# One of four tiles of exponentials folded on GpSimd before VectorE adds it

## The chip, the cores and the metric

The kernel runs on one core of one Trainium2 chip. A core has a matrix engine (TensorE, PE in the profile), and VectorE (DVE), ScalarE (ACT) and GpSimd (POOL), each with an instruction queue of its own that it works off in order; a further queue (SP) only issues transfers (DMA). The metric is the device time of one execution in microseconds. "The profile" is a recording of one execution with the start and the duration of every instruction.

## The reference

An input `x` of 2048 tokens by 512 is normalised. From it come an attention over cached keys and values (32 heads of 128, 2048 queries, 2048 keys) and a small network that makes a gate; the output is `x + attention * silu(network)`.

```python
def _A_ref(x, k_cache, v_cache, wq, wo):
    q = (x @ wq).reshape(B, Sq, H, Dh).transpose(0, 2, 1, 3)
    scores = jnp.einsum("bhqd,bhkd->bhqk", q, k_cache) * (Dh ** -0.5)
    p = _softmax(scores, axis=-1)
    o = jnp.einsum("bhqk,bhkd->bhqd", p, v_cache)
    return o.transpose(0, 2, 1, 3).reshape(B, Sq, H * Dh) @ wo

xn = _layernorm(x, axis=-1)
s = _A_ref(xn, A_k_cache, A_v_cache, A_wq, A_wo)
g = _silu(_B_ref(xn, B_w1, B_w2, B_w3, B_w4))
return x + s * g
```

What matters here is the denominator of the softmax: for every query the sum of the exponentials over all 2048 keys.

## The kernel before

The network runs first, in about the first 155 us. The rest is the attention, cut into 128 *units*: one head by one block of 512 queries (8 groups of 4 heads, 4 blocks of queries per group, the heads of a group next to each other). A unit has 8 *slots*, `n = 8 * u + p` with `p` the slot in unit `u`. A slot multiplies two blocks of 128 keys with the queries (`s_slot`, L425; out comes a 128x1024 block of scores, keys in the partitions), and ScalarE writes their exponentials (L436) into half of a tile `pT` of 128 x 4 x 512. So a unit has four such tiles, the second full after slot 3, the third after slot 5, the fourth after slot 7. There are six buffers for them. Ten slots behind, `pv_slot` multiplies the tiles with the values.

**The sums.** VectorE adds the four tiles into one accumulator `acc` of the same shape: tiles 0 and 1 in slot 4 (`add_first`, L442), tile 2 in slot 6 (`add_next`, L447), tile 3 in slot 0 of the next unit (L447 as well). The accumulator is then halved twice (`fold`, L451, to 1024 columns; `fold_last`, L455, to 512), turned by a transposing DMA (`turn`, L480), summed along the columns (`turned_sums`, L485), inverted (L491), and sent through DRAM to all partitions (`dr`, then `rb`). In slot 7 of the second unit after it, `norm` (L509) multiplies the attention's output in PSUM with it.

**The queries.** From unit 16 on the queries of two heads (a *pair*: an even and an odd unit) are made with seven smaller products in place of eight (`product`, L367), whose results VectorE combines in four steps, `q_part` 0 to 3 (L413, L416, L418, L421). They share one PSUM tile per pair, `ps_q`: after `q_part` 1 and 2, in slots 0 to 1 of the odd unit, the next two products (slots 4 and 5) write into the same tile, and `q_part` 3 in slot 6 reads it.

**The output product.** `wo_slot` multiplies finished heads with `wo` into a PSUM bank `ps_wo`, which `wo_post` (L571, or L564 and others for the last groups) adds to a running result on VectorE; the bank is then free for the next one. In the last groups VectorE also scales and adds up results (L537, L542, L567, L580, L582).

**What sets the order.** Every instruction is pinned in the order of the program's text, so that each engine's queue is fixed by the loop over `n` (L932 to L1002). In slot 0 of a unit VectorE's queue holds: `turned_sums`, the reciprocal, `add_next(u - 1, 3)`. Then, in slot 0 or 1: `q_part(1)`, `fold`, `q_part(2)`, `fold_last` in odd units; `fold`, `q_part(0)`, `fold_last` spread over slots 0 to 2 in even ones. GpSimd's queue holds only work of the first 155 us, among it the `rs` powers (L194). A small pool `pS` has, under the tag `tm`, two buffers of 2 KB per partition that `wo_post` uses for intermediate results in the last two groups.

Of the kernel before, what the change touches and what calls it, by code (L numbers as in the profile page):

```python
# [9 lines left out]
ALU = mybir.AluOpType  # L10
FP32 = mybir.dt.float32
BF16 = mybir.dt.bfloat16
# [5 lines left out]
def kernel(  # L18
# [15 lines left out]
    nc = tc.nc  # L34
    P = nc.NUM_PARTITIONS
# [15 lines left out]
    HG = 4  # L51
# [10 lines left out]
    pin = tc.keep_in_program_order  # L62
# [48 lines left out]
    def mm(out, lhsT, rhs, start, stop, **kw):  # L111
# [9 lines left out]
        out=ident[:], in0=diag[:], scalar1=0.0, scalar2=None, op0=ALU.is_equal))  # L121
# [9 lines left out]
    kTs, vBs, wqs, wos, oTs, st = {}, {}, {}, {}, {}, {}  # L131
# [183 lines left out]
    def q_mm(u, dcs, tag="xa"):  # L315
        g, qt, hh = units[u]
        if dcs[0] == 0:
            st[u] = dict(psq=psX.tile([P, 512], FP32, tag=tag, name="ps_q"))
        for dc in dcs:
            mm(st[u]["psq"][:], wqs[g * HG + hh][:, dc, :],  # L320
               xnT[:, dc, qt * 512:(qt + 1) * 512], dc == 0, dc == DC - 1)
# [85 lines left out]
    def q_part(v, i):  # L407
        s = sw[v]
        ps = turned(v, s["ps"][:])
        t = lambda: q_tile(v, pS, dtype=FP32, tag="tq", bufs=3, name="tq")  # L410
        if i == 0:
            s["u"] = t()
            pin(nc.vector.tensor_tensor(out=s["u"][:], in0=ps[:, 1], in1=s["m1"][:], op=ALU.add))  # L413
        elif i == 1:
            s["u3"] = t()
            pin(nc.vector.tensor_tensor(out=s["u3"][:], in0=ps[:, 0], in1=s["u"][:], op=ALU.add))  # L416
        elif i == 2:
            pin(nc.vector.tensor_tensor(out=s["q"][:, 3], in0=ps[:, 1], in1=s["u3"][:], op=ALU.add))  # L418
        else:
            u = s["u"][:].unsqueeze(1)  # L420
            pin(nc.vector.tensor_tensor(  # L421
                out=s["q"][:, 1:3], in0=ps, in1=u.to_broadcast([P, 2] + list(u.shape[2:])), op=ALU.add))
            del sw[v]

    def s_slot(u, p):  # L425
        g, qt, hh = units[u]
        s = st[u]
        sps = psS.tile([P, 2, 512], FP32, name="ps_s")
        for j in range(2):
            kc = 2 * p + j  # L430
            kv = kTs[g * HG + hh].rearrange("d (i p j) -> d i j p", p=P, j=KJ)
            mm(sps[:, j, :], kv[:, kc // KJ, kc % KJ, :], s["qT"], True, True)
        if p % 2 == 0:
            s.setdefault("pT", []).append(pB.tile([P, 4, 512], BF16, tag="pT", bufs=6, name="pT"))
        jj = 2 * (p % 2)
        pin(nc.scalar.activation(  # L436
            out=s["pT"][-1][:, jj:jj + 2, :], in_=sps[:], func=ACT.Exp, scale=SCALE))

    def add_first(u):
        s = st[u]  # L440
        s["acc"] = pB.tile([P, 4, 512], BF16, tag="acc", bufs=2, name="acc")
        pin(nc.vector.tensor_tensor(  # L442
            out=s["acc"][:], in0=s["pT"][0][:], in1=s["pT"][1][:], op=ALU.add))

    def add_next(u, i):
        a = st[u]["acc"]
        pin(nc.vector.tensor_tensor(out=a[:], in0=a[:], in1=st[u]["pT"][i][:], op=ALU.add))  # L447

    def fold(u):
        a = st[u]["acc"]  # L450
        pin(nc.vector.tensor_tensor(out=a[:, 0:2, :], in0=a[:, 0:2, :], in1=a[:, 2:4, :], op=ALU.add))  # L451

    def fold_last(u):
        a = st[u]["acc"]
        pin(nc.vector.tensor_tensor(out=a[:, 0, :], in0=a[:, 0, :], in1=a[:, 1, :], op=ALU.add))  # L455
# [22 lines left out]
    def turn(u):  # L478
        st[u]["tT"] = pB.tile([P, 4, P], BF16, tag="tT", bufs=2, name="tT")
        pin(nc.sync.dma_start_transpose(out=st[u]["tT"][:], in_=st[u]["acc"][:, 0, :]))  # L480

    def turned_sums(u):
        s = st[u]
        sm = s["sm"] = smp.tile([P, 4], FP32, name="sm")
        pin(nc.vector.tensor_reduce(out=sm[:], in_=s["tT"][:], axis=mybir.AxisListType.X, op=ALU.add))  # L485

    def turned_recip(u):
        s = st[u]
        sm = s["sm"]
        rc = smp.tile([P, 4], FP32, name="rc")  # L490
        pin(nc.vector.reciprocal(out=rc[:], in_=sm[:]))  # L491
        s["dr"] = drp.tile([P, 4], FP32, name="dr")
        pin(nc.sync.dma_start(out=s["dr"][:], in_=rc[:]))

    def bcast(u):
        st[u]["rb"] = pB.tile([P, 512], FP32, tag="rb", bufs=2, name="rb")
        pin(nc.sync.dma_start(
            out=st[u]["rb"][:], in_=st[u]["dr"][:].rearrange("p j -> (p j)").partition_broadcast(P)))
# [335 lines left out]
    pS = None  # L834
# [36 lines left out]
    def pv_run(n):  # L871
        while pv_at[0] <= n - LAG:
            pv_slot(*divmod(pv_at[0], SPU))
            pv_at[0] += 1
# [9 lines left out]
    UA, UB = NU - 2, NU - 1  # L884

    def wo_slot(part, n, each=2, **kw):
        gg, t = wo_todo[0]
        if part < HG // each:
            wo_mm(gg, t, tuple(range(part * each, (part + 1) * each)), **kw)
            return  # L890
        wo_todo.popleft()
        wo_post(gg, t, n)
        if gg == NG - 1 and t % 4 < 3 and t + 1 not in fin and t // 4 not in LATE:
            fin_load(t + 1)

    FIRST, LAST = 16, NU - 4
    pairs = range(FIRST, LAST + 1, 2)
    q_plan = defaultdict(list)
    steps = defaultdict(list)
    first, third = {}, {}  # L900
    for v in pairs:
        a = (v - 2) * SPU
# [8 lines left out]
    def fold_at(u):  # L911
        return 1 if u in third else 0

    def run_steps(n, which):
        for fn, v, k in steps.get(n, ()):
            if fn is which:
                fn(v, k)
# [4 lines left out]
    for h in range(HG, H, 2):  # L922
        u = (h // HG) * QT * HG + (-4, -2)[h % HG // 2]
# [8 lines left out]
    for n in range(UB * SPU):  # L932
        u, p = divmod(n, SPU)
        extra = len(wo_todo) > 1 and u in (2 * HG, 2 * HG + 1)
        if p == 0 and wo_box:
            wo_slot(4, n, each=1)
        s_slot(u, p)
        pv_run(n)
        for v, dcs in q_plan.get(n, ()):
            q_mm(v, dcs)  # L940
        run_steps(n, product)
        run_steps(n, q_take)
        if p == 0 and 1 <= u:
            if u - 2 in TURN:
                turned_sums(u - 2)
                turned_recip(u - 2)
            add_next(u - 1, 3)
        if p == 1 and u - 2 in TURN:
            bcast(u - 2)
        if p == fold_at(u) and 1 <= u:  # L950
            for v in third.get(u, ()):
                q_part(v, 1)
            fold(u - 1)
            for v in third.get(u, ()):
                q_part(v, 2)
            if u != UA and u not in first:
                fold_last(u - 1)
        if p == 2 and u in first:
            q_part(first[u], 0)
            fold_last(u - 1)  # L960
        if p == 3 and u - 1 in TURN:
            turn(u - 1)
        if p == 0:
            twice = extra
        if twice and p < 3:
            wo_slot(p, n, tag="xa")
        for v, k in ((u + 1, 3), (u + 2, 7)):
            if p == k and "psq" in st.get(v, ()) and (k == 3) == (v > FIRST):
                q_copy(v)
        if u - 2 in TURN:  # L970
            norm_p, sum_p, wo_p, each = 7, 5, 3, 1
        else:
            norm_p, sum_p, wo_p, each = 4, 5, 4, 1
        at_wo = [wo_p + i for i in range(HG // each + 1)]
        if FIRST - 2 <= u < LAST:
            at_wo = ([1, 3, 4, 6, 7], [0, 2, 3, 6, 7])[u % 2]
        if p == norm_p and 2 <= u and not u - 2 in TURN:
            norm_queue(u - 2)
        if p == sum_p and 1 <= u and u - 1 not in TURN:
            sums(u - 1)  # L980
        if p == sum_p + 1 and 1 <= u and u - 1 not in TURN:
            bcast(u - 1)
        if u == UA and p in (1, 2, 3):
            wo_slot(p - 1, n)
            if p == 3:
                fold_last(u - 1)
        if p in at_wo and wo_todo and pS is not None and (p == at_wo[0] or wo_box):
            wo_slot(at_wo.index(p), n, each=each)
        if p == norm_p and u - 2 in TURN:
            norm_queue(u - 2)  # L990
        run_steps(n, q_part)
        if p == 4:
            add_first(u)
        if p == 6:
            add_next(u, 2)
        pay()
        held_mm(n)
        for fn in todo.pop(n, ()):
            fn()
        if pS is None and not held:  # L1000
            right.close()
            pS = right.enter_context(pool("pS", side="right", reuse_waits="tile"))  # L1002
# [31 lines left out]
    def pv_to(k):  # L1034
# [29 lines left out]
        out=diag[:], in0=diag[:], scalar1=0.0, scalar2=None, op0=ALU.is_equal))  # L1064
# [98 lines left out]
```

## Time and profile before

| | |
|---|---|
| median of 3 runs | 1235.81 us (1235.81 to 1235.9) |
| the profiled execution | 1236.42 us |
| its span, first to last instruction | 1234.6 us |
| TensorE busy | 1227.5 us (99%) |
| ScalarE busy | 1105.8 us (90%) |
| VectorE busy | 1030.1 us (83%) |
| GpSimd busy | 26.6 us (2%) |
| granted TensorE clock | 1.00 |
| the units 24 to 124 | from about 331 to 1196 us |

A row of the groups reads: line, engine, operation, tile written and tiles read, shapes, count, then the time that the group kept its engine busy and the mean duration in ns, then the time that the engine stood idle before these instructions and what ended it. A row of the waits reads: who waited, for whom, the sum in us, how often, the longest. A row of the timeline reads: start and duration in us, then as above; in brackets the idle time before it. Matmuls overlap one another: a 128x512 one is shown with 0.38 us, while in the middle of the kernel one starts about every 0.22 us.

### The profile page before, as it was taken

Reading aid. Unit: us, or ns where it says so; the run is one execution under the profiler, and the core shown is the slowest. Engines: PE = TensorE matmul, PEld = TensorE weight load, DVE = VectorE, ACT = ScalarE, POOL = GpSimd, SP = SyncE. Lnnn points to the kernel's source line nnn. Section 1 sums busy time; section 2 is a strip of 40 time slices with the busy share of each in tenths; the row PEclk is TensorE's granted clock in tenths of the full one; section 3 lists DMA queues with packets and bytes.
Section 4 is the critical chain, followed back from the end, with each engine's and each line's share of the span. In section 5 each row is a group of like instructions: output and inputs, shape, how many; then the busy total and the mean of one; then the engine's idle time right before and its main releaser. Section 6 shows DMA issues by size and latency. Waiting matters only on the chain.

```text
span 1234.6 us, 17534 instructions
## 1 busy us (share of the span) xinstructions
PE 1227.5 (99%) x6267; PEld 636.5 (52%) x6267; DVE 1030.1 (83%) x1647; ACT 1105.8 (90%) x1237; POOL 26.6 (2%) x75
## 2 busy tenths in 40 slices
PE   9999999999999999999999999999999999999998
PEld 6444444455555555555555555555555555555545
DVE  7712778899888888988889888888889999999997
ACT  6345999899999999999999999999999999999996
POOL 5300000000000000000000000000000000000000
PEclk9999999999999999999999999999999999999999
DMA  8661122664334423354243523543345424553342
GB/s 176 168 140 35 31 39 65 96 99 94 63 80 100 106 57 82 87 111 85 58 95 91 111 56 69 103 104 72 76 83 111 107 58 90 99 107 66 77 81 66
DMA packets 244056, 107.75 MB, mean 87 GB/s; under 512 B 194816, under 2 KB 227712, under 8 KB 243968
## 3 DMA queue, kind: packets, MB, share of 16 engines
q1 hardware_dynamic: 243408, 106.17, 41.5%
q8 instruction: 49, 0.80, 0.3%
q10 hardware_dynamic: 560, 0.46, 0.1%
q14 instruction: 39, 0.32, 0.1%
HBM read 67.50 MB, written 2.36 MB: 57 GB/s over the span
## 4 chain that ended last, share of the span: by engine, by line
PE 94%; DVE 3%; DMA 2%; ACT 1%; issue 0%; SPq 0%; DVEq 0%; ACTq 0%
PE ps_s L112 39%; PE ps_o L112 37%; PE ps_wo L112 8%; PE ps_q L112 8%; PE ps_m L112 2%; DMA tT<-acc 1%; DVE acc L447 1%; ACT pT L436 1%; DMA rb<-dr 0%; DMA xin<-in_A_x_dram 0%; DVE sm L485 0%; PE ps_oh L112 0%; DVE oT L509 0%; DVE acc L451 0%; DVE y L1025 0%
## 5 line engine op out<-in xcount | busy, mean ns | idle before, releaser
L436 ACT ACTIVATE pT<-ps_s 128x1024 bf16<-128x1024 f32 x1016 | 1016.2, 1025 | 56.8 <-PE ps_s L112 26.1
L112 PE MATMUL ps_s<-qT,kT 128*128 128x512 bf16 (+1 forms) x2064 | 609.3, 378 | 0.0
L112 PE MATMUL ps_o<-pT,vb 128*128 128x512 bf16 x1984 | 590.2, 379 | 0.0
L447 DVE TENSOR_TENSOR acc<-acc,pT 128x2048 bf16<-128x2048 bf16 x254 | 307.0, 1208 | 54.9 <-ACT pT L436 54.4
L112 PEld LDWEIGHTS <-kT 128*128 128x128 bf16 x2064 | 232.7, 113 | 151.3 <-issue 1.0
L112 PEld LDWEIGHTS <-vb 128*128 128x128 bf16 x1984 | 193.9, 98 | 216.6
L442 DVE TENSOR_TENSOR acc<-pT 128x2048 bf16<-128x2048 bf16 x127 | 155.4, 1224 | 38.4 <-ACT pT L436 35.5
L112 PE MATMUL ps_wo<-wo_h,oT 128*128 128x512 bf16 x496 | 186.3, 379 | 0.0
L451 DVE TENSOR_TENSOR acc<-acc 128x1024 bf16<-128x1024 bf16 x127 | 87.4, 688 | 2.5
L509 DVE TENSOR_TENSOR oT<-ps_o,rb 128x512 bf16<-128x512 f32 x127 | 86.6, 682 | 1.1 <-DMA rb<-dr 0.8
L485 DVE TENSOR_REDUCE sm<-tT 128x4 f32<-128x512 bf16 x124 | 83.9, 676 | 2.8 <-DMA tT<-acc 2.7
L112 PEld LDWEIGHTS <-oT 128*128 128x128 bf16 x528 | 51.4, 98 | 52.6 <-issue 0.6
L112 PEld LDWEIGHTS <-wc 128*128 128x128 bf16 x440 | 43.0, 98 | 54.1 <-issue 2.7
L571 DVE TENSOR_TENSOR sacc<-ps_wo,sacc 128x512 f32<-128x512 f32 x96 | 65.7, 684 | 0.0
L112 PEld LDWEIGHTS <-wq_h 128*128 128x128 bf16 x398 | 38.9, 98 | 46.3
L112 PE MATMUL ps_q<-xnT,wq_h 128*128 128x256 bf16 (+1 forms) x288 | 61.1, 298 | 0.4 <-DVE sacc L559 0.4
L421 DVE TENSOR_TENSOR qT<-ps_q,tq 128x512 bf16<-128x512 f32 x55 | 38.0, 692 | 23.3 <-PE ps_q L112 22.9
L455 DVE TENSOR_TENSOR acc<-acc 128x512 bf16<-128x512 bf16 x127 | 52.9, 417 | 0.5
L293 ACT ACTIVATE h2T<-ps_s 128x1024 bf16<-128x1024 f32 x28 | 28.6, 1023 | 25.9 <-PE ps_s L112 25.9
L112 PE MATMUL ps_s<-xn2T,w_sb 128*128 128x512 bf16 x224 | 48.8, 379 | 0.0
L112 PEld LDWEIGHTS <-w_sb 128*128 128x128 bf16 x368 | 33.5, 98 | 29.6
L112 PE MATMUL ps_q<-xs,wc 128*128 128x256 bf16 x246 | 47.0, 273 | 0.0
(102 smaller groups left out, 585.6 us busy)
## 6 DMA issues: line engine op xcount, KB each, us to landing
rb<-dr SPq DMA_DIRECT2D x127, 256.0 KB, 3.9
vb<-in_A_v_cache_dram SPq DMA_DIRECT2D x62, 256.0 KB, 3.0
wq_h<-in_A_wq_dram SPq DMA_DIRECT2D x32, 128.0 KB, 3.0
wo_h<-in_A_wo_dram SPq DMA_DIRECT2D x32, 128.0 KB, 2.5
w_sb<-in_B_w_dram SPq DMA_DIRECT2D x8, 256.0 KB, 5.0
kT<-in_A_k_cache_dram SPq DMA_TRANSPOSE x128, 2.8
xl<-in_A_x_dram SPq DMA_DIRECT2D x16, 128.0 KB, 3.0
dr<-rc SPq DMA_DIRECT2D x127, 2.0 KB, 1.4
```

Of the source, the lines that this page charges most:

```text
L112: pin(nc.tensor.matmul(out=out, lhsT=lhsT, rhs=rhs, start=start, stop=stop, **kw))
L293: pin(nc.scalar.activation(out=h2[c, f][:], in_=ps[:], func=ACT.Gelu_apprx_tanh))
L421: pin(nc.vector.tensor_tensor(out=s["q"][:, 1:3], in0=ps, in1=u.to_broadcast([P, 2] + list(u.shape[2:])), op=ALU.add))
L436: pin(nc.scalar.activation(out=s["pT"][-1][:, jj:jj + 2, :], in_=sps[:], func=ACT.Exp, scale=SCALE))
L442: pin(nc.vector.tensor_tensor(out=s["acc"][:], in0=s["pT"][0][:], in1=s["pT"][1][:], op=ALU.add))
L447: pin(nc.vector.tensor_tensor(out=a[:], in0=a[:], in1=st[u]["pT"][i][:], op=ALU.add))
L451: pin(nc.vector.tensor_tensor(out=a[:, 0:2, :], in0=a[:, 0:2, :], in1=a[:, 2:4, :], op=ALU.add))
L455: pin(nc.vector.tensor_tensor(out=a[:, 0, :], in0=a[:, 0, :], in1=a[:, 1, :], op=ALU.add))
L485: pin(nc.vector.tensor_reduce(out=sm[:], in_=s["tT"][:], axis=mybir.AxisListType.X, op=ALU.add))
L509: pin(nc.vector.tensor_tensor(out=to, in0=o, in1=rb, op=ALU.mult))
L571: pin(nc.vector.tensor_tensor(out=sa, in0=ps[:], in1=sa, op=ALU.add))
```

## The change

For units 24 to 124 (`APART`) the second tile of exponentials, tile 1, is no longer added by VectorE as a whole. In slot 4 GpSimd adds its two halves (columns 0 to 1023 and 1024 to 2047) into a new tile `ph` of 1024 columns, which takes its buffer under the tag `tm`. VectorE's first add moves to slot 6 and adds tiles 0 and 2. In slot 0 of the next unit, ahead of the add of tile 3, VectorE adds `ph` to the first half of the accumulator. Later the accumulator's halves are added to each other as before, so the sum is the same apart from rounding. Units before 24 and after 124 are left as they were. The order of all other instructions on every engine stays.

```diff
-    def add_first(u):
+    def add_first(u, i=1):
         s = st[u]
         s["acc"] = pB.tile([P, 4, 512], BF16, tag="acc", bufs=2, name="acc")
         pin(nc.vector.tensor_tensor(
-            out=s["acc"][:], in0=s["pT"][0][:], in1=s["pT"][1][:], op=ALU.add))
+            out=s["acc"][:], in0=s["pT"][0][:], in1=s["pT"][i][:], op=ALU.add))
+
+    def add_aside(u):
+        s = st[u]
+        s["ph"] = pS.tile([P, 2, 512], BF16, tag="tm", bufs=2, name="ph")
+        pin(nc.gpsimd.tensor_tensor(
+            out=s["ph"][:], in0=s["pT"][1][:, 0:2, :], in1=s["pT"][1][:, 2:4, :], op=ALU.add))
+
+    def add_join(u):
+        a = st[u]["acc"]
+        pin(nc.vector.tensor_tensor(
+            out=a[:, 0:2, :], in0=a[:, 0:2, :], in1=st[u].pop("ph")[:], op=ALU.add))
...
+    APART = range(FIRST + 2 * HG, UA - 1)
...
+            if u - 1 in APART:
+                add_join(u - 1)
             add_next(u - 1, 3)
...
         if p == 4:
-            add_first(u)
-        if p == 6:
+            (add_aside if u in APART else add_first)(u)
+        if p == 6 and u in APART:
+            add_first(u, 2)
+        elif p == 6:
             add_next(u, 2)
```

## The prediction

> **What bounds the kernel now.** I read four views of the stretch in which the edited units lie, from 331 to 1196 us (it holds the 101 units that the change touches): busy time by engine, the waits, the groups of VectorE, and the timeline of one pair of units. Busy time first (columns: length, then PE, weight loads, VectorE, ScalarE, GpSimd, granted clock, DMA):
>
> ```profile
> 331.00:1196.00 865.00, 863.40 (x4344) 448.76 (x4343) 768.91 (x1198) 825.39 (x910) 0.00 (x0) 1.00 0.41 87
> ```
>
> TensorE is idle for 865.00 - 863.40 = 1.6 us. So what sets the time here is TensorE's stream, and VectorE, with 865.00 - 768.91 = 96.1 us idle, is not the bound. GpSimd does nothing at all. The waits of the same stretch say what VectorE's idle time is:
>
> ```profile
> DVE acc L447 <- ACT pT L436: 40.9, 50, 0.9
> DVE qT L421 <- PE ps_q L112: 22.0, 44, 0.5
> ...
> PE ps_q L112 <- DVE qT L418: 1.4, 3, 1.0
> ```
>
> Two thirds of it (62.9 us) is waiting for the exponentials of slot 6 or for a product; the rest is mostly in slot 4, before the first add. TensorE waited for VectorE three times, always in the same place: the next query product after q_part(2) (L418). That place matters below. Now one pair of units as VectorE sees it (start, duration), an odd unit's slots 4 to 6 and then an even unit's slot 4 to the next odd unit's slot 1, and two late q_part(2):
>
> ```profile
> 703.99 1.23 DVE L442 TENSOR_TENSOR acc<-pT 128x2048 bf16<-128x2048 bf16 x1 [0.54 <-ACT pT L436]
> 705.74 0.69 DVE L421 TENSOR_TENSOR qT<-ps_q,tq 128x512 bf16<-128x512 f32 x1 [0.53 <-PE ps_q L112]
> 706.35 1.22 DVE L447 TENSOR_TENSOR acc<-acc,pT 128x2048 bf16<-128x2048 bf16 x1
> ...
> 712.41 1.23 DVE L442 TENSOR_TENSOR acc<-pT 128x2048 bf16<-128x2048 bf16 x1 [0.34 <-ACT pT L436]
> 714.57 1.23 DVE L447 TENSOR_TENSOR acc<-acc,pT 128x2048 bf16<-128x2048 bf16 x1 [0.93 <-ACT pT L436]
> 715.71 0.68 DVE L571 TENSOR_TENSOR sacc<-ps_wo,sacc 128x512 f32<-128x512 f32 x1
> 716.32 0.68 DVE L509 TENSOR_TENSOR oT<-ps_o,rb 128x512 bf16<-128x512 f32 x1
> 716.91 0.68 DVE L485 TENSOR_REDUCE sm<-tT 128x4 f32<-128x512 bf16 x1
> 717.62 0.18 DVE L491 RECIPROCAL rc<-sm 128x4 f32<-128x4 f32 x1
> 717.72 1.19 DVE L447 TENSOR_TENSOR acc<-acc,pT 128x2048 bf16<-128x2048 bf16 x1
> 718.83 0.42 DVE L416 TENSOR_TENSOR tq<-ps_q,tq 128x256 f32<-128x256 f32 x1
> 719.16 0.68 DVE L451 TENSOR_TENSOR acc<-acc 128x1024 bf16<-128x1024 bf16 x1
> 719.76 0.42 DVE L418 TENSOR_TENSOR qT<-ps_q,tq 128x256 bf16<-128x256 f32 x1
> ...
> 942.55 0.42 DVE L418 TENSOR_TENSOR qT<-ps_q,tq 128x256 bf16<-128x256 f32 x1
> ...
> 1183.91 0.42 DVE L418 TENSOR_TENSOR qT<-ps_q,tq 128x256 bf16<-128x256 f32 x1
> ```
>
> And the TensorE instructions that use what VectorE frees there, in order of time:
>
> ```profile
> 716.99 0.38 PE L112 MATMUL ps_wo<-wo_h,oT 128*128 128x512 bf16 x1
> ...
> 721.31 0.27 PE L112 MATMUL ps_q<-xnT,wc 128*128 128x256 bf16 x1
> ...
> 943.29 0.38 PE L112 MATMUL ps_q<-xnT,wc 128*128 128x256 bf16 x2
> ...
> 1184.38 0.38 PE L112 MATMUL ps_q<-xnT,wc 128*128 128x256 bf16 x2
> ```
>
> Two slacks come out of this. wo_post ends at 715.71 + 0.68 = 716.39, and the next wo matmul, which needs that bank, runs at 716.99: 0.60 us. q_part(2) ends at 720.18 and the product behind it runs at 721.31: 1.13 us. The second slack is smaller late in the kernel, where VectorE also updates the result: 943.29 - 942.97 = 0.32 us in the first of the last 15 pairs, 1184.38 - 1184.33 = 0.05 us in the last; those 15 have 0.29 us on the mean.
>
> **The change, part by part.** *VectorE.* Durations of the adds:
>
> ```profile
> L447 DVE TENSOR_TENSOR acc<-acc,pT 128x2048 bf16<-128x2048 bf16 x203 | 245.2, 1208 | 41.0 <-ACT pT L436 40.9
> L442 DVE TENSOR_TENSOR acc<-pT 128x2048 bf16<-128x2048 bf16 x101 | 123.6, 1224 | 24.3 <-ACT pT L436 21.9
> L451 DVE TENSOR_TENSOR acc<-acc 128x1024 bf16<-128x1024 bf16 x101 | 69.4, 688 | 1.7
> ```
>
> Each of 101 units loses a 128x2048 add (1.208) and gains a 128x1024 add of the folded half (the join, 0.688, the row of the fold of that shape): 101 x 0.520 = 52.5 us less VectorE work. None of it is on TensorE's stream. More than that, it is removed in slot 4, and VectorE waits in slot 6 for the third tile of exponentials anyway (0.93 us at 714.57). From 714.57 to q_part(2) it has no idle time, and there the join is added: sm, rc, join, last add, q_part(1), fold, q_part(2). So q_part(2) comes 0.69 us later, where 1.13 us or, late, 0.29 us are free. Of the saved time nothing reaches the place where VectorE is looked for.
>
> *The first add* moves from slot 4 to slot 6 and joins tiles 0 and 2; the accumulator is taken two slots later. Cost nothing: a tile's buffer is written again 12 slots on, and 8 slots are the 8.2 us from the add of 706.35 to that of 714.57; the add of tile 0 comes some 6 us before that. The same cover holds for ScalarE, whose exponentials now also wait until GpSimd has read tile 1.
>
> *GpSimd's add*, 128x1024, is new; its queue is empty here (0.00 above), so nothing of its own stands behind it. Nothing of that size runs on GpSimd before. The nearest rows, and VectorE's work beside the last of them:
>
> ```profile
> 0.82 0.24 POOL L118 IOTA diag<- 128x128 f32 x1 [0.39 <-POOLq L1147]
> 1.00 0.10 POOL L684 MEMSET hT<- 128x3 bf16 x1
> ...
> 51.94 0.57 POOL L194 TENSOR_TENSOR rs<-ve,nhalf 128x1 f32<-128x1 f32 x1
> ...
> 52.79 0.74 POOL L194 TENSOR_TENSOR rs<-ve,nhalf 128x1 f32<-128x1 f32 x1
> ```
>
> ```profile
> 52.79 2.00 DVE L219 TENSOR_SCALAR xn<-xall,mv,rs 128x512 bf16<-128x512 bf16 x6
> ```
>
> From memset to iota, 125 more elements cost 0.14 us, 1.1 ns each, for one stream. Estimate for 1024 elements: 0.10 + 1.16 = 1.3 us if the two inputs and the output stream together, 2.4 us if the two inputs come in turn, 3.6 us if all three do. I take 2.4, the middle, and keep 1.3 and 3.6 as ends. (The Trainium skill, GPSIMD Engine Reference, § 3.1, has 4497 ns for an fp32 add of 2048 elements and gives the two inputs in turn as the reason; half of it is an estimate of 2.25 us, by which the sum below would be +44 instead of +59 us.)
>
> *What the two engines do to each other* decides the rest. The only row that bears on it is the last GpSimd row: the same instruction that takes 0.57 took 0.74 us when VectorE started a run of adds and scalings on SBUF tiles at the same moment. I take it that a GpSimd add and a VectorE add of two SBUF tiles do not run side by side: whichever starts second waits. (By the Trainium skill, SBUF — State Buffer, § Who interferes with whom, a VectorE instruction with two SBUF inputs contends with a GpSimd instruction that reads SBUF, and the pair of ports is held for a whole instruction; the 0.17 us agrees in direction only, since the row beside it has one tile as input.)
>
> Then the sum is a ring. In the 865 us VectorE has 96.1 us of idle time and gains 52.5: 148.6 us. GpSimd's adds take 101 x 2.4 = 242.4 us. They lie between the second tile's exponentials and VectorE's first add, and beside them VectorE can do only q_part(3) of each odd unit (L421, reads PSUM): 50 x 0.69 = 34.5 us. So 242.4 - 34.5 = 207.9 us have to fit into 148.6: TensorE is held up for about 59 us. One pair by hand shows where. Even unit: GpSimd runs 712.41 to 714.81; the first add, which before had its tile at 714.57, is 0.24 late; with the join q_part(2) is 0.93 late, inside 1.13, and the last fold too. In the odd unit GpSimd then starts late itself (its tile at 703.99, VectorE idle 0.54 before), by 0.4, and ends at 706.8, so the add of 706.35 is 0.4 late; the next join makes that 1.1 and GpSimd starts 0.8 late in the even unit. Now its add there is 1.0 late and wo_post with it, against 0.60: TensorE waits 0.4 us for the wo bank, and with the next join another 0.2 for q_part(2). That is 0.6 to 0.7 us a pair in steady state, some 33 us over 50 pairs; the pairs that also load weights or update results have less idle time, which the ring's 59 counts.
>
> *DMA and SP.* The transposing DMA of the sums is issued behind the last fold, so up to 1 us later, and what SP has queued behind it too. I cost it at nothing because the reduction that reads it is late by about as much; where that cover fails a unit pays at most the join's 0.69 us.
>
> Sum: 1236.4 (the profiled execution) + 59 = 1295 us; that execution is 0.6 us above the median of 1235.81, so 1295 stands for either.
>
> **The rivals.** *Side by side.* The engines do not hinder each other, or the add takes 1.3 us: 131 - 34.5 = 97 us fit into 148.6 with room. Then only the join counts: of 50 pairs the 35 early ones hide 0.69 us in 0.9 to 1.13, the 15 late ones pay 0.69 - 0.29 = 0.40 each: +6 us, 1242. For it: the one row on interference shows 0.17 us only. Against it: that row shows some.
>
> *GpSimd's streams all in turn*, 3.6 us, in series: 363.6 - 34.5 - 148.6 = +180 us, 1416. Against it: nothing but the estimate.
>
> *Not slower, perhaps faster.* In the late pairs VectorE may be so far behind that it does not wait in slot 6; the 0.52 us saved then reaches q_part(2), and the three waits go. It decides if slot 6 of those units is without a wait for exponentials; the wait row has 50 such waits in 50 pairs, which speaks against. Its worth ends at TensorE's idle time: 1.6 us, 1234.8. That is inside 0.2% (2.5 us), about what a measurement of this kernel can tell from no change.
>
> **How the numbers follow.** In series with an add of 2 to 2.8 us: 0.53; longer adds in series: 0.08; side by side or a short add: 0.29; not slower: 0.10, of which 0.03 faster by over 0.2%, for which idle time outside the stretch would have to go too. The likeliest gives 1295; each 0.1 us of the add is 10 us, so 2.0 us gives 1255 and 2.8 us 1335. The range takes in the side-by-side case from 1240 and ends at 1335.
>
> **What would show it.** In series: GpSimd busy about 240 us in the stretch; VectorE's add of slot 6 starting where GpSimd's add ends, in both units of a pair; new waits of TensorE for wo_post (L571's place) above all and for q_part(2); about 0.7 us or more of TensorE idle time in each pair. Side by side: the slot-6 add keeps its wait for exponentials, the product behind q_part(2) waits in the last 15 pairs alone. The prediction is wrong if GpSimd's add is shorter than 1.8 us, where the ring closes, or if VectorE's adds run on through it.

## The result

The changed kernel takes 1308.2 us (median of 6 runs, 1301.7 to 1311.2) against 1235.8 before: ratio 1.058, 95% interval 1.0565 to 1.0593. That is 72 us more; 1295 in a range of 1240 to 1335 was forecast.

Busy time of the changed kernel in the stretch with the 101 units, now 937 us long (331 to 1268; columns as before: length, TensorE, weight loads, VectorE, ScalarE, GpSimd, granted clock, DMA):

```profile
331.00:1268.00 937.00, 879.59 (x4265) 452.30 (x4347) 837.30 (x1198) 828.68 (x911) 231.06 (x101) 0.99 0.37 80
```

TensorE is idle for 57 us of it instead of 1.6, and the granted clock is 0.99 instead of 1.00. GpSimd is busy for 231 us. VectorE has 52 us less to do by its instructions and is busy for 68 us *more*. The groups say which instructions grew (line, engine, operation, count, busy us, mean ns, idle before):

```profile
L448 POOL TENSOR_TENSOR ph<-pT 128x1024 bf16<-128x1024 bf16 x101 | 231.1, 2288 | 980.4 <-ACT pT L436 849.3
...
L458 DVE TENSOR_TENSOR acc<-acc,pT 128x2048 bf16<-128x2048 bf16 x153 | 186.7, 1220 | 26.0 <-ACT pT L436 15.5
L442 DVE TENSOR_TENSOR acc<-pT 128x2048 bf16<-128x2048 bf16 x127 | 155.7, 1226 | 42.1 <-ACT pT L436 41.5
L466 DVE TENSOR_TENSOR acc<-acc 128x512 bf16<-128x512 bf16 x127 | 129.3, 1018 | 0.5
L462 DVE TENSOR_TENSOR acc<-acc 128x1024 bf16<-128x1024 bf16 x127 | 120.3, 947 | 2.5
```

The two folds (L462 was L451, L466 was L455) take 947 and 1018 ns on the mean where they took 688 and 417. Their instructions are the same; the time is waiting inside the instruction, which the profile counts as busy. The big adds are as long as before. The waits of TensorE in the changed kernel:

```profile
PE ps_q L112 <- DVE qT L418: 40.2, 24, 3.2
PE ps_q L112 <- DVE tq L413: 10.6, 6, 2.0
PE ps_o L112 <- DVE oT L520: 1.2, 3, 0.6
...
PE ps_wo L112 <- DVE sacc L582: 0.5, 2, 0.3
```

So TensorE waits for `q_part(2)` (24 times, 1.7 us on the mean) and `q_part(0)`, hardly ever for `wo_post`. One such wait, by VectorE, then ScalarE and GpSimd, then TensorE (timeline of the changed kernel):

```profile
1012.70 1.23 DVE L458 TENSOR_TENSOR acc<-acc,pT 128x2048 bf16<-128x2048 bf16 x1
1013.84 0.68 DVE L548 SCALAR_TENSOR_TENSOR sacc<-sacc,xall 128x512 f32<-128x512 f32 x1
1014.45 0.42 DVE L416 TENSOR_TENSOR tq<-ps_q,tq 128x256 f32<-128x256 f32 x1
1014.78 2.51 DVE L462 TENSOR_TENSOR acc<-acc 128x1024 bf16<-128x1024 bf16 x1
1017.21 0.41 DVE L418 TENSOR_TENSOR qT<-ps_q,tq 128x256 bf16<-128x256 f32 x1
```

```profile
1013.53 1.02 ACT L436 ACTIVATE pT<-ps_s 128x1024 bf16<-128x1024 f32 x1
...
1014.63 2.11 POOL L448 TENSOR_TENSOR ph<-pT 128x1024 bf16<-128x1024 bf16 x1 [6.32 <-ACT pT L436]
```

```profile
1017.68 0.38 PE L112 MATMUL ps_q<-xnT,wc 128*128 128x256 bf16 x2 [2.68 <-DVE qT L418]
```

GpSimd starts 0.08 us after the last exponentials of its tile (1013.53 + 1.02 = 1014.55). It does so in the other units too: 0.08 to 0.13 us after them in all 101, whatever VectorE is doing. VectorE is late here and still ahead of its folds, in `q_part(1)` (L416), which reads PSUM and one SBUF tile. The fold that comes next, 0.69 us of work, finds GpSimd's add running; it lasts until GpSimd is done at 1016.74 and its own work after that. `q_part(2)` stands behind the fold in VectorE's queue, and TensorE behind `q_part(2)`.

Which of the two engines waits depends on which comes first. Two other units show it (the fold and GpSimd's add):

```profile
410.47 0.69 DVE L462 TENSOR_TENSOR acc<-acc 128x1024 bf16<-128x1024 bf16 x1
410.48 2.67 POOL L448 TENSOR_TENSOR ph<-pT 128x1024 bf16<-128x1024 bf16 x1 [6.04 <-DVE acc L458]
...
715.14 2.12 POOL L448 TENSOR_TENSOR ph<-pT 128x1024 bf16<-128x1024 bf16 x1 [6.62 <-ACT pT L436]
715.21 2.59 DVE L462 TENSOR_TENSOR acc<-acc 128x1024 bf16<-128x1024 bf16 x1
```

At 410 us the fold is first by 0.01 us: it keeps its 0.69 us, and GpSimd's add lasts 2.67 us instead of 2.12, its time undisturbed (below). At 715 us GpSimd is first by 0.07 us: its add keeps 2.12 us, and the fold lasts 2.59. (The profile names L458 for the start at 410.48 because its end was the last event before it; the exponentials of that tile ended at 410.40.) In the stretch 19 folds and 47 last folds are held up in this way, by up to 1.9 us each and by 33 and 76 us in sum. Behind 18 of the 19 folds TensorE waits 1.6 to 3.2 us, 45 us in sum. A last fold has neither `q_part(2)` nor `q_part(0)` behind it.

### The profile page after: what moved, and what is told of

It reads as the page before. It is cut to its first block, busy times and chain, and to the rows that moved or that the text cites. A ratio compares the mean times of both kernels' runs of the same rounds, so it can differ in the third digit from the quotient of the medians.

```text
span 1307.3 us, 17616 instructions
## 1 busy us (share of the span) xinstructions
PE 1241.8 (95%) x6149; PEld 640.1 (49%) x6267; DVE 1099.4 (84%) x1647; ACT 1108.1 (85%) x1237; POOL 257.6 (20%) x176
## 4 chain that ended last, share of the span: by engine, by line
PE 52%; DVE 34%; DMA 6%; issue 3%; ACT 2%; SPq 1%; DVEq 0%; ACTq 0%
PE ps_s L112 22%; PE ps_o L112 19%; DVE acc L458 6%; DVE acc L466 5%; PE ps_q L112 5%; DMA tT<-acc 4%; PE ps_wo L112 4%; DVE acc L462 4%; DVE sm L496 3%; DVE acc L442 3%; DVE acc L453 3%; PE ps_m L112 2%; ACT pT L436 2%; DVE oT L520 2%; DMA rb<-dr 1%
## 5 line engine op out<-in xcount | busy, mean ns | idle before, releaser
L112 PE MATMUL ps_o<-pT,vb 128*128 128x512 bf16 x1906 | 577.1, 381 | 4.4 <-DVE oT L520 0.8
L448 POOL TENSOR_TENSOR ph<-pT 128x1024 bf16<-128x1024 bf16 x101 | 231.1, 2288 | 980.4 <-ACT pT L436 849.3
L458 DVE TENSOR_TENSOR acc<-acc,pT 128x2048 bf16<-128x2048 bf16 x153 | 186.7, 1220 | 26.0 <-ACT pT L436 15.5
L112 PE MATMUL ps_wo<-wo_h,oT 128*128 128x512 bf16 x475 | 179.4, 381 | 0.6 <-DVE sacc L582 0.5
L466 DVE TENSOR_TENSOR acc<-acc 128x512 bf16<-128x512 bf16 x127 | 129.3, 1018 | 0.5
L462 DVE TENSOR_TENSOR acc<-acc 128x1024 bf16<-128x1024 bf16 x127 | 120.3, 947 | 2.5
L112 PE MATMUL ps_q<-xnT,wc 128*128 128x256 bf16 x194 | 37.8, 277 | 40.7 <-DVE qT L418 40.2
L421 DVE TENSOR_TENSOR qT<-ps_q,tq 128x512 bf16<-128x512 f32 x55 | 37.7, 686 | 41.6 <-PE ps_q L112 41.6
L453 DVE TENSOR_TENSOR acc<-acc,ph 128x1024 bf16<-128x1024 bf16 x101 | 66.7, 660 | 0.0
L293 ACT ACTIVATE h2T<-ps_s 128x1024 bf16<-128x1024 f32 x28 | 28.6, 1023 | 25.9 <-PE ps_s L112 25.2
```

Source lines behind the costliest of these rows:

```text
L112: pin(nc.tensor.matmul(out=out, lhsT=lhsT, rhs=rhs, start=start, stop=stop, **kw))
L421: pin(nc.vector.tensor_tensor(out=s["q"][:, 1:3], in0=ps, in1=u.to_broadcast([P, 2] + list(u.shape[2:])), op=ALU.add))
L448: pin(nc.gpsimd.tensor_tensor(out=s["ph"][:], in0=s["pT"][1][:, 0:2, :], in1=s["pT"][1][:, 2:4, :], op=ALU.add))
```

## The experiments

The theory, A: a GpSimd add and a VectorE add of two SBUF tiles do not run side by side, whoever is second waits to the end of the other's instruction. Rivals: B, the order of the adds costs (the join ahead of `q_part(2)`, the first add moved); C, any work of GpSimd costs, wherever it stands; D, the two share a port bit by bit rather than by whole instructions.

**The same order without GpSimd.**

```diff
     def add_aside(u):
...
-        pin(nc.gpsimd.tensor_tensor(
+        pin(nc.vector.tensor_tensor(
             out=s["ph"][:], in0=s["pT"][1][:, 0:2, :], in1=s["pT"][1][:, 2:4, :], op=ALU.add))
```

> The changed kernel with the fold of tile 1 done by VectorE instead of GpSimd, at the same place in the order: same tiles, same join, no GpSimd. Theory A (the two engines' reads of SBUF exclude each other): only the late place of the join is left, 0.69 us against the slack before the product behind q_part(2), so 1238 to 1248 us, folds L462 and L466 back at 0.69 and 0.42 us. Rival B (the new order of the adds, with the join in slot 0, is what costs): 1290 to 1310 us as in the changed kernel, since VectorE has 101 x 0.69 = 69 us more to do than there.

Measured: 1248.7 us beside 1237.4 before, ratio 1.0088 (1.0073 to 1.0103). So 61 of the 72 us need GpSimd, although VectorE here does all that GpSimd did. The other 11 are rival B's, and sit where the prediction put them:

```profile
PE ps_q L112 <- DVE qT L418: 9.6, 15, 1.3
```

15 waits, as many as there are late pairs with little slack; where +6 us were worked out, the change of order costs 11.

**GpSimd's add beside the kernel before,** its result unread.

```diff
         if p == 4:
+            if u in APART:
+                add_aside(u)
             add_first(u)
```

> The kernel before, all adds on VectorE, and GpSimd's fold of tile 1 beside it in units 24 to 124, whose result nothing reads. Theory A: VectorE's work is not relieved, so GpSimd's 231 us, less 34 us beside q_part(3), must fit into 96 us of VectorE's idle time: about 100 us more than before, 1310 to 1350 us, with folds or adds stretched by up to 2.3 us. Rival B (the order of the adds costs): 1236 us, since VectorE's order is that of before and nothing waits for GpSimd.

Measured: 1311.4 us, ratio 1.0597 (1.0579 to 1.0615), +74. Nothing waits for GpSimd's result and VectorE's program is the one of before, so B cannot explain it. The groups (VectorE's first add, last fold, first fold, from 331 us on):

```profile
L442 DVE TENSOR_TENSOR acc<-pT 128x2048 bf16<-128x2048 bf16 x103 | 160.1, 1555 | 0.4 <-ACT pT L436 0.3
L461 DVE TENSOR_TENSOR acc<-acc 128x512 bf16<-128x512 bf16 x103 | 114.3, 1109 | 0.1
L457 DVE TENSOR_TENSOR acc<-acc 128x1024 bf16<-128x1024 bf16 x104 | 71.5, 687 | 1.8
```

Here it is the first add and the last fold that wait, TensorE waits for `wo_post` (46 times, 42 us in sum), and the granted clock is 1.00. I had expected some 100 us; with an add of 2.12 us (below) in place of 2.3 the same working gives 214 - 34 - 96 = 84.

**GpSimd writes, and reads only one element.** Its add becomes a copy of one element, which keeps the start, and two memsets of the tile. The sum of the exponentials leaves out tile 1 here.

```diff
-        pin(nc.gpsimd.tensor_tensor(
-            out=s["ph"][:], in0=s["pT"][1][:, 0:2, :], in1=s["pT"][1][:, 2:4, :], op=ALU.add))
+        pin(nc.gpsimd.tensor_copy(out=s["ph"][:, 0, 0:1], in_=s["pT"][1][:, 3, 511:512]))
+        pin(nc.gpsimd.memset(s["ph"][:], 0.0))
+        pin(nc.gpsimd.memset(s["ph"][:], 0.0))
```

> The changed kernel with GpSimd's add replaced by a copy of one element of tile 1 (which keeps the start where it was) and two memsets of the 128x1024 tile; the sum of the exponentials lacks tile 1, VectorE's instructions are the same. Theory A in its narrow form (only GpSimd's reading of SBUF is in the way): 1238 to 1248 us and folds of 0.69 and 0.42 us. Rival C (any work of GpSimd on SBUF holds VectorE up for as long as it lasts): 1280 to 1315 us if the memsets take some 2 us together, with the folds stretched.

Measured: 1248.3 us, ratio 1.0088, the same as without GpSimd. GpSimd is busy as long as in the changed kernel, and the folds are back:

```profile
L449 POOL MEMSET ph<- 128x1024 bf16 x101 | 96.2, 952 | 6.0
L450 POOL MEMSET ph<- 128x1024 bf16 x101 | 96.2, 952 | 5.8
L448 POOL COPY ph<-pT 128x1 bf16<-128x1 bf16 x101 | 36.7, 363 | 911.0 <-ACT pT L436 904.5 <-DVE acc L459 6.5
```

```profile
L463 DVE TENSOR_TENSOR acc<-acc 128x1024 bf16<-128x1024 bf16 x104 | 71.5, 687 | 1.9
L467 DVE TENSOR_TENSOR acc<-acc 128x512 bf16<-128x512 bf16 x104 | 43.2, 416 | 0.1
```

So it is GpSimd's reading of SBUF that is in the way, not its being busy. C falls. (That is what the Trainium skill, SBUF — State Buffer, § Who interferes with whom, states: a VectorE instruction with two SBUF inputs contends with a GpSimd instruction that reads SBUF, not with one that only writes it. These runs agree, at 61 us for the one and none for the other.)

**The add in two halves.**

```diff
-        pin(nc.gpsimd.tensor_tensor(
-            out=s["ph"][:], in0=s["pT"][1][:, 0:2, :], in1=s["pT"][1][:, 2:4, :], op=ALU.add))
+        for i in range(2):
+            pin(nc.gpsimd.tensor_tensor(
+                out=s["ph"][:, i, :], in0=s["pT"][1][:, i, :], in1=s["pT"][1][:, 2 + i, :], op=ALU.add))
```

> The changed kernel with GpSimd's add cut into two adds of 128x512, one behind the other. Theory A, with a hold that lasts one instruction: a fold that meets GpSimd waits for at most 1.2 us instead of 2.3, the waits behind q_part(2) become about half as long and no halved clock follows them; 1265 to 1295 us. Rival D (the two share the port element by element, or the wait goes on while GpSimd has anything queued): folds still stretched to 2 us and more, 1300 to 1315 us.

Measured: 1270.2 us, ratio 1.0275 (1.0261 to 1.0289), half of the loss. GpSimd does the same work in smaller pieces, and TensorE's wait behind `q_part(2)` is half as long in sum (20.7 us for 40.2), and the longest is 1.9 us instead of 3.2:

```profile
PE ps_q L112 <- DVE qT L418: 20.7, 17, 1.9
...
PE ps_q L112 <- DVE tq L413: 3.6, 5, 0.9
```

The folds of this kernel (count, then the shortest, the median and the longest in ns):

```profile
L463 DVE TENSOR_TENSOR acc<-acc x127: 679/691/1686, 130.3 to 1249.1; 128x1024 bf16<-128x1024 bf16 x127
L467 DVE TENSOR_TENSOR acc<-acc x127: 411/1040/1382, 131.0 to 1249.8; 128x512 bf16<-128x512 bf16 x127
```

The longest fold is held up by 1.0 us, about as long as one half add (1.14 us at the shortest), where it was 1.9 in the changed kernel. So VectorE gets in between GpSimd's two adds, and the hold lasts one instruction. D falls.

**GpSimd held back until the last fold is done.**

```diff
+        late = smp.tile([P, 1], BF16, tag="late", bufs=2, name="late")
+        pin(nc.gpsimd.tensor_copy(out=late[:], in_=st[u - 1]["acc"][:, 0, 0:1]))
         pin(nc.gpsimd.tensor_tensor(
```

> The changed kernel with GpSimd held back until VectorE's last fold of the unit before is done (it first copies one element of that result). Theory A: no fold is stretched any more, VectorE's first add in slot 6 waits for GpSimd instead, and TensorE waits for wo_post, 0.6 to 0.7 us a pair, the place that the prediction gave; 1265 to 1295 us, no halved clock. Rival D: the same as the changed kernel, 1300 to 1315 us.

Measured: 1299.1 us, ratio 1.0512 (1.0497 to 1.0526). That is above the range that was expected (1265 to 1295), but the pattern is the expected one: `wo_post` (L584, L577 here) is now the first thing that TensorE waits for.

```profile
PE ps_wo L112 <- DVE sacc L584: 23.9, 44, 1.1
PE ps_q L112 <- DVE qT L418: 12.9, 15, 1.2
PE ps_wo L112 <- DVE tm L577: 4.2, 4, 1.2
```

VectorE's first add, 1.22 us of work, now waits for GpSimd: GpSimd ends at 704.60 + 2.12 = 706.72, and the add 1.08 us later, at 706.16 + 1.64 = 707.80:

```profile
704.60 2.12 POOL L450 TENSOR_TENSOR ph<-pT 128x1024 bf16<-128x1024 bf16 x1
```

```profile
706.16 1.64 DVE L442 TENSOR_TENSOR acc<-pT 128x2048 bf16<-128x2048 bf16 x1
```

Undisturbed, GpSimd's add takes 2.12 us.

**The third tile in place of the second.** GpSimd folds tile 2 in slot 6, and VectorE adds tiles 0 and 1 in slot 4 as before. Beside GpSimd then stand `wo_post`, `norm`, the reduction and the reciprocal, with one SBUF tile or none.

```diff
-            out=s["ph"][:], in0=s["pT"][1][:, 0:2, :], in1=s["pT"][1][:, 2:4, :], op=ALU.add))
+            out=s["ph"][:], in0=s["pT"][2][:, 0:2, :], in1=s["pT"][2][:, 2:4, :], op=ALU.add))
...
-            (add_aside if u in APART else add_first)(u)
+            add_first(u)
         if p == 6 and u in APART:
-            add_first(u, 2)
+            add_aside(u)
```

> Tile 2 is folded by GpSimd in slot 6 instead of tile 1 in slot 4: VectorE adds tiles 0 and 1 in slot 4 as before, then has wo_post, norm, the reduction and the reciprocal (2.0 us, one SBUF tile or none each), then the join. Theory A: GpSimd's 2.3 us lie beside those, nothing of VectorE with two SBUF tiles is due, so little or nothing is left: 1233 to 1245 us, GpSimd still busy for 230 us. Rival C (GpSimd's work costs wherever it stands): 1280 us or more.

Measured: 1258.8 us, ratio 1.0174 (1.0159 to 1.0189). 221 us of GpSimd's adds now cost 21 us and not 72, but the time is above the 1233 to 1245 us that were expected. What was left I split into the join's place and the VectorE work that still has two SBUF tiles.

**The join behind `q_part(2)`,** without GpSimd and with the third tile.

```diff
-            if u - 1 in APART:
-                add_join(u - 1)
             add_next(u - 1, 3)
...
             if u != UA and u not in first:
+                if u - 1 in APART:
+                    add_join(u - 1)
                 fold_last(u - 1)
...
```

> No GpSimd (VectorE folds tile 1 itself), and the join moved from slot 0 to behind q_part(2) and q_part(0), just ahead of the last fold. If the 11 us of the same kernel with the early join are the join's place ahead of q_part(2): 1236 to 1241 us, TensorE's waits behind q_part(2) back at 1 to 3 us. If they are VectorE's larger amount of work (101 x 0.17 = 17 us more than before): 1245 to 1250 us still.

> GpSimd folds tile 2 in slot 6, and the join stands behind q_part(2). If the join's place is what is left of the 21 us of the same kernel with the early join, some 10 us of it go: 1243 to 1250 us. If both places were the whole of it, 1234 to 1240 us. If the join's place does not matter: 1258 us.

Measured: 1237.5 us without GpSimd, ratio 1.0012 (1.0003 to 1.0021): the 11 us were the join's place ahead of `q_part(2)`, not VectorE's larger amount of work. With the third tile on GpSimd 1246.7 us, ratio 1.0085 (1.0072 to 1.0099): 10 of its 21 us go as well. The rest shows in its groups; each of these took 0.29 or 0.69 us before and reads two SBUF tiles in slots 6 and 7:

```profile
L365 DVE TENSOR_TENSOR wc<-wq_h,wc 128x256 bf16<-128x256 bf16 x24 | 36.0, 1501 | 0.0
L591 DVE SCALAR_TENSOR_TENSOR xall<-sacc,xall 128x512 bf16<-128x512 f32 x8 | 11.2, 1404 | 0.3
L578 DVE TENSOR_TENSOR sacc<-sacc,tm 128x512 f32<-128x512 f32 x8 | 10.0, 1244 | 0.3
```

**Those weight differences moved ahead of GpSimd's add,** and then the two late updates (L537, L542) out of slot 0 as well, the latter also in the kernel before alone.

```diff
-            at((u + i // 2) * SPU + (2, 6)[i % 2], lambda h=h, i=i: w_sum(h, i))
+            at((u + i // 2) * SPU + (2, 5)[i % 2], lambda h=h, i=i: w_sum(h, i))
...
-            at(k, lambda: y_scale(t))
-            at(k + SPU, lambda: y_add(t))
+            at(k + 5, lambda: y_scale(t))
+            at(k + SPU + 5, lambda: y_add(t))
```

> GpSimd folds tile 2, late join, and the weight differences (L365) of slot 6 moved to slot 5, ahead of GpSimd's add. With them behind it, 24 of them took 1.5 us on the mean instead of 0.29. Theory A: they are back at 0.29 us, and most of the 10 us that this kernel still had go: 1237 to 1242 us. Rival: they were hidden anyway, and the 10 us come from the result's updates that read two SBUF tiles in the last groups (L578, L591): 1244 to 1247 us.

> The same with the two late updates moved to slot 5 as well. Theory A: VectorE has 52 us less work than before and nothing of it stands beside GpSimd's add but L578 and L591: 1233 to 1240 us, at best 0.2% less than before, since TensorE had only 2 to 3 us of idle time to give.

> The kernel before, without GpSimd, with the two late updates of the result (L537, L542; 16 instructions of 0.69 us) moved from slot 0, ahead of q_part(1), to slot 5, where VectorE waits for exponentials. If the place ahead of q_part(2) is what costs, TensorE's 1.4 us of waits there go: 1233 to 1235 us beside 1235.9, that is 0.1% less at most; if not, no change.

Measured: 1242.4 us beside 1237.0, ratio 1.0045 (1.0032 to 1.0058), with the weight differences moved, just above what was expected (0.445 us each on the mean, so some still meet GpSimd); 1242.6, ratio 1.0040 (1.0027 to 1.0054), with both moved: no further gain, a miss. The kernel before with the late updates alone moved: 1235.7, ratio 0.9990 (0.9981 to 0.9998), as expected: TensorE's three waits behind `q_part(2)` (1.4 us) become one of 0.4 us. No form with GpSimd's add beat the kernel before. Of the last 5 us, 3.4 are two waits of TensorE behind `q_part(3)` (L421), which the kernel before does not have: a moved weight difference meets GpSimd's add, and `q_part(3)` stands behind it (timeline and waits of the kernel with the weight differences moved):

```profile
1065.62 2.37 POOL L448 TENSOR_TENSOR ph<-pT 128x1024 bf16<-128x1024 bf16 x1 [7.29 <-ACT pT L436]
1065.93 2.21 DVE L365 TENSOR_TENSOR wc<-wq_h,wc 128x256 bf16<-128x256 bf16 x1
...
PE ps_s L112 <- DVE qT L421: 3.4, 2, 1.7
```

What the rest is was not settled.

## Why the prediction was right

The direction and the cause came out: slower, because a GpSimd add and a VectorE add of two SBUF tiles exclude each other. The size, 72 us where 59 were forecast, came out by luck (*The ring*, below), and the place of the waits did not. The side-by-side rival is what the first and the third experiment made by other means, 11 us and not 6. Step by step:

- *The exclusion.* Right, though the prediction had little for it. Next to its row of 0.74 us stands another of the same instruction, at 53.65 us, that took 0.58 us inside the same run of VectorE (52.79 to 54.79 us).
- *VectorE's work off the path.* Right: 52 us less of it brought nothing, and TensorE's idle time before was the ceiling. Even the best arrangement with GpSimd stayed above the kernel before.
- *The join's place.* Right in mechanism and number of pairs (15), too small: 11 us instead of 6. The working took only the 0.69 us against the slack; that the transposed sums, too, come later was put at nothing. In the first experiment VectorE waits 1.01 us for them just ahead of TensorE's longest wait (1.26 us); how much of the other 5 us this is was not measured.
- *GpSimd's add.* 2.4 us was taken; 2.12 us undisturbed, 2.29 on the mean here. (The Trainium skill, GPSIMD Engine Reference, § 3.1, gives 4497 ns for 2048 fp32 elements. Half, 2.25 us, is an estimate that comes closer than mine.) By 10 us for each 0.1 us the sum was 28 us too high from this term.
- *The ring.* Wrong as a sum, and close only because its errors had opposite signs. It let GpSimd's time fill all of VectorE's idle time; VectorE still has 937.0 - 837.3 = 100 us of it in the stretch, since a wait at a bad place does not use up idle time elsewhere. With 2.12 us the ring would have given some 31 us. That 59 came near 72 is luck.
- *Where TensorE waits.* Wrong. "New waits of TensorE for `wo_post` above all": 0.5 us. The hand-worked pair made the last fold late and let GpSimd start only when that was done, so that the first add of slot 6 would wait. But GpSimd's start hangs on its tile alone, 0.08 us behind the exponentials. It is the folds, late by the join and by earlier holds, that come second, in 18 cases with `q_part(2)` or `q_part(0)` and TensorE behind them; the first add took 1.23 us on the mean, as before. So there are 18 waits of 1.6 to 3.2 us rather than one of 0.7 in every pair. Holding GpSimd back until after the fold brought the predicted waits, and 1299 us.
- *DMA and SP.* Not seen to matter by itself: VectorE's wait for the turned sums went from 2.2 us in the stretch to 5.8.

One term was missing altogether, the clock. The changed kernel's granted clock around one of the long waits:

```profile
1053.00:1057.00 4.00, 1.81 (x9) 0.74 (x8) 4.00 (x4) 2.39 (x3) 2.11 (x1) 1.00 0.38 66
1057.20:1060.60 3.40, 3.11 (x10) 1.43 (x10) 0.92 (x3) 1.02 (x1) 0.00 (x0) 0.51 0.24 56
1061.00:1065.00 4.00, 3.95 (x20) 2.04 (x20) 3.86 (x7) 3.98 (x5) 0.00 (x0) 1.00 0.09 24
```

After a wait of 2.68 us TensorE ran at half its clock for 3.4 us. The trace has eight such stretches before the kernel's last microseconds, each at the end of a wait of 2.0 to 3.2 us or up to 1.3 us behind it: 8 x 3.4 / 2 = 14 us. (TensorE's busy time in the stretch rose by 879.6 - 863.4 = 16 us.) So the 72 us are 11 of the join's place, some 14 of the halved clock, and the remaining 47 of waiting for the shared access; the last is a difference and not measured by itself. The 18 waits behind a held fold sum to 45 us, but the join's lateness is in some of them too. The kernels with two halves and with GpSimd held back, whose longest waits behind `q_part(2)` are 1.9 and 1.2 us, have a granted clock of 1.00.

## What to carry to other kernels

An idle GpSimd is no free help for VectorE where both read SBUF: its add held up a VectorE instruction with two SBUF tiles that came second by up to 1.9 us, and the loss was set by what stood behind that instruction in VectorE's queue. GpSimd starts when its input is there, so ask where VectorE will be at that moment, late as it may be by then. If work goes there at all, put it beside VectorE instructions that read PSUM or one tile, and cut it into short instructions. And where one engine's stream is full (here 1.6 us idle in 865), relief of another can bring no more than that, and a new place in the order can cost far more.

## What the runs showed of the hardware that was not expected

- The first to come holds the access for its whole instruction, and 0.07 us are enough: GpSimd's add of 715.14 went ahead of the fold of 715.21, though that followed straight on another VectorE add of two SBUF tiles. The fold waited 1.9 us.
- The wait does not show as idle time. It lengthens the waiting instruction, so VectorE's busy time rose by 68 us with 52 us less work; a group whose mean has grown without a change of shape is the sign.
- Waits of TensorE of 2.0 to 3.2 us were followed, in eight cases, by 3.4 us at half the clock; six others, of 2.7 to 3.0 us, were not. (The Trainium skill, TensorE: Matmul & The Clock Gate, Part 1, tells of a free-running window of about 3.4 us over which activity is judged. That would fit the length and that only some waits trigger it; no run here separates it from other reasons.)
- Two memsets of 128x1024 on GpSimd, 0.95 us each, cost VectorE nothing.
